# The wait at the end of a one-core transformer block: the wait for all stores on GpSimd's queue instead of SyncE's

## The chip, the cores and the metric

One core of one Trainium2 chip runs the whole kernel as one program. The metric is device time in microseconds (us). The times of before are three: 149.34 us median, 149.03 lowest, 149.63 highest. The profiled execution took 149.33 us.

## The reference

A layer norm of `x` (2048 tokens, 448 features) feeds two branches, and both are added to `x`. All tensors are bfloat16.

```python
xn = _layernorm(x, axis=-1)
return x + _A_ref(xn, A_wqkv, A_w_phi, A_wo) + _B_ref(xn, B_w1, B_b1, B_w2)
```

Branch A is a linear attention with 16 heads of 28 features: `q`, `k` and `v` come from one projection, `q` and `k` pass through a small matrix per head, and the feature map is the softmax of that and of its negative. Numerator and denominator are sums over all tokens, their quotient goes through `wo`. Branch B is a dense layer of 448 to 1792 features with bias, a Mish activation, and a dense layer back to 448.

## The kernel before, in words

The 2048 tokens stand as 16 tiles of 128 tokens. Layer norm runs on pairs of tiles; the normalised pairs are transposed; TensorE makes `k`, `v` and `q` of each pair and the first dense layer (`ffn1`); ScalarE applies the exponentials and Mish; GpSimd scales the feature map of `k`; then TensorE makes numerator and denominator of each tile (`nd`), the projection by `wo` (L845) and the second dense layer (`ffn2`, L828). The last two add into the same PSUM bank of a tile. VectorE adds that bank to `x` (L793) and writes the sum into the tile `x_all`, from where it is stored. The order of the whole program is written out by hand in a list of step names (`ORDER`), whose end is `... g15 stt14 sto6 stt15`: `g15` is the second dense layer of token tile 15, `stt14` the store of tile 14, `sto6` that of tiles 12 and 13, `stt15` that of tile 15.

Tile 15 is the last one. Its columns 0 to 383 are made first; its columns 384 to 447 come from 18 narrow matmuls behind them (L807 to L810, `last_columns`), and VectorE adds these with an instruction of its own (L814). It is therefore stored in two pieces: the first by ScalarE's DMA queue, the second by SyncE's (L856). All other stores are issued by SyncE (L859). There are ten stores: `sto0` to `sto6`, `stt14`, and the two of `stt15`.

Each operation is recorded with what it reads and writes. `resolve` works out from that which earlier operations each one must wait for; each DMA has a semaphore of its own, which its landing raises to 16. `emit` then writes the engines' programs: for each operation its waits, and then the instruction itself.

```python
    def emit(self, name, eng):
        for o in self.ops[name]:
            for d in o.deps:
                eng.wait_ge(d.sem, d.count)
            ins = o.fn(eng)
```

The waits are L131 in the profile. The last recorded operation, behind the whole order, is an empty one on SyncE that reads everything the ten stores wrote (L928). So it waits for ten semaphores. In the built program that is five instructions of SyncE's queue that each wait for two semaphores; four of them count as L131, and the fifth, which waits for the two stores of tile 15, as L928. There is no further instruction for the empty operation. SyncE's last other instruction is the store of tile 15's last columns (L856). GpSimd's last instruction is a copy of 64 by 64 elements (L820), which waits for two loads of `wo` and which one of the narrow matmuls reads (L808).

When an engine has come to the end of its program, the engines meet: the trace holds the times at which one more semaphore, number 2, is raised, which the kernel does not use. It is raised in rounds of nine: two rounds ahead of the program's first instruction, and two around and behind its last.

Of the kernel before, what the change touches and what calls it, by code (L numbers as in the profile page):

```python
# [17 lines left out]
NT = S // P  # L18
# [20 lines left out]
class Program:  # L39
# [13 lines left out]
    def op(self, eng, fn, r=(), w=(), dma=False, tag="", after=()):  # L53
        o = Op()
        o.tag, o.parts = tag, None
        o.eng, o.fn, o.dma, o.needed, o.count, o.sem = eng, fn, dma, False, 0, None
        o.idx = len(self.ops[eng])
        deps = list(after)
        for res in list(r) + list(w):
            if res[0] == "ps":  # L60
                deps += [a for e, a in self.psum.get(res, {}).items() if e != eng]
        for res in r:
            if res[0] != "ps":
                deps += self.writers.get(res, [])
        for res in w:
            if res[0] != "ps":
                deps += [d for d in self.writers.get(res, []) if d.dma or dma or d.eng != eng]
                deps += [d for d in self.readers.get(res, []) if d.dma or dma or d.eng != eng]
        for res in r:
            if res[0] == "ps":  # L70
                self.psum.setdefault(res, {})[eng] = o
            else:
                self.readers.setdefault(res, []).append(o)
        for res in w:
            if res[0] == "ps":
                self.psum.setdefault(res, {})[eng] = o
            else:
                self.writers[res] = [o]
                self.readers[res] = []
        o.deps = deps  # L80
        self.ops[eng].append(o)
        self.order = getattr(self, "order", [])
        self.order.append(o)
        return o
# [54 lines left out]
def bass_parallel_sum__linear_kernel_hedgehog__dense_activation_mish__prompt_kernel(  # L139
    nc, A_x, A_wqkv, A_w_phi, A_wo, B_x, B_w1, B_b1, B_w2, out  # L140
):
    es = ExitStack()
    with es:
        _kernel(es, nc, A_x, A_wqkv, A_w_phi, A_wo, B_w1, B_b1, B_w2, out)
# [21 lines left out]
def run_order(steps, order):  # L166
    for name in order:
        steps[name]()


def _kernel(es, nc, A_x, A_wqkv, A_w_phi, A_wo, B_w1, B_b1, B_w2, out):
# [88 lines left out]
    op, dma = pg.op, pg.dma  # L260
# [508 lines left out]
    LAST = int(ORDER.split()[-1][3:])  # L769
# [155 lines left out]
        add(f"z{n}", warm, n)  # L925

    run_order(steps, ORDER.split())
    op("SP", lambda e: e.nop(), r=[("dram", t) for t in range(NT)] + [("draml", LAST)])  # L928

    pg.resolve()  # L930
    for name, eng in (("SP", nc.sync), ("POOL", nc.gpsimd), ("PE", nc.tensor), ("ACT", nc.scalar), ("DVE", nc.vector)):
# [29 lines left out]
```

## Time and profile before

| | |
|---|---|
| median of three runs | 149.34 us (149.03 to 149.63) |
| the profiled execution | 149.33 us |
| its span, first to last recorded instruction | 148.1 us |
| instructions in it | 3852 |
| TensorE matmul busy | 143.2 us (97%) |
| VectorE busy | 102.8 us (69%) |
| ScalarE busy | 74.5 us (50%) |
| GpSimd busy | 38.7 us (26%) |
| granted TensorE clock | 1.00 |

The page calls TensorE's matmuls PE, VectorE DVE, ScalarE ACT, GpSimd POOL and SyncE SP. A q behind a name is the engine's sequencer, which waits on semaphores and issues DMAs; its instructions do not count as busy time. The span ends with the last recorded instruction, so the profiled execution has 1.2 us outside of its span, ahead of the first instruction or behind the last.

### The profile page before, as it was taken

What the parts mean: (1) busy time and instruction counts of PE and PEld (TensorE: products, weight loads), DVE (VectorE), ACT (ScalarE), POOL (GpSimd) and SP (SyncE); (2) the same over time, 40 slices, a digit from 0 to 9 for tenths busy, and PEclk for the clock granted to TensorE, in tenths of its full rate; (3) what the DMA queues carried; (4) which work ended last, traced back from release to release, by engine and by line L of the source; (5) the groups of instructions that cost most, each with busy time, mean ns of one, the idle gap of its engine ahead of it and who ended that gap; (6) DMA issues with size and microseconds to landing.
All of it is one profiled execution on the core that took longest, in us unless ns stands there. A gap on an engine that the chain in (4) does not pass through costs nothing.

```text
span 148.1 us, 3852 instructions
## 1 busy us (share of the span) xinstructions
PE 143.2 (97%) x1669; PEld 75.3 (51%) x1669; DVE 102.8 (69%) x229; ACT 74.5 (50%) x91; POOL 38.7 (26%) x53
## 2 busy tenths in 40 slices
PE   6799999999999999999999999999999999999994
PEld 2375555465554554444444455545555555555473
DVE  0699898996999940407698879639993999940062
ACT  4987999869999999657756753003000000000000
POOL 4414465179999993000000000000000000000000
DMA  4997777799699179399956033020004050533005
GB/s 133 243 284 221 155 143 150 118 170 328 112 192 188 37 40 145 63 228 309 194 121 127 0 66 62 12 55 0 7 2 122 0 128 0 124 62 124 4 0 186
DMA packets 39965, 17.23 MB, mean 116 GB/s; under 512 B 33933, under 2 KB 39181, under 8 KB 39949
## 3 DMA queue, kind: packets, MB, share of 16 engines
q1 hardware_dynamic: 39776, 16.89, 54.6%
q8 instruction: 13, 0.21, 0.6%
q10 hardware_dynamic: 172, 0.10, 0.2%
q14 instruction: 4, 0.02, 0.1%
HBM read 7.02 MB, written 1.84 MB: 60 GB/s over the span
## 4 chain that ended last, share of the span: by engine, by line
PE 93%; DMA 2%; DVE 1%; ACT 1%; POOL 1%; issue 0%
PE PS L423 51%; PE PS L828 29%; PE PS L845 7%; PE PS L722 3%; DMA x_all<-in_A_x_dram 2%; PE PS L649 2%; PE PS L580 1%; DVE xn L497 1%; PE PS L505 1%; ACT junk L458 1%; POOL rstd L473 0%; ACT junk L453 0%; DVE x_all L793 0%; PE PS L556 0%; POOL lnv L470 0%
## 5 line engine op out<-in xcount | busy, mean ns | idle before, releaser
L423 PE MATMUL PS<-xnT,W 64*128 64x512 bf16 x392 | 44.8, 377 | 0.0
L828 PE MATMUL PS<-W,actT 128*128 128x448 bf16 (+1 forms) x224 | 42.9, 351 | 0.0
L699 ACT ACTIVATE actT<-PS,b1T 128x1024 bf16<-128x1024 f32 x28 | 29.8, 1112 | 22.1 <-PE PS L423 22.1
L828 PEld LDWEIGHTS PS<-W,actT 128*128 128x128 bf16 x224 | 21.5, 98 | 19.8 <-issue 0.3
L423 PEld LDWEIGHTS PS<-xnT,W 64*128 64x128 bf16 x392 | 18.4, 94 | 21.5 <-PE PS L423 1.9
L630 POOL TENSOR_TENSOR actT<-actT,rSk 128x896 bf16<-128x896 bf16 x16 | 26.6, 1699 | 5.3 <-DVE rSk L628 5.3
L793 DVE TENSOR_TENSOR x_all<-PS,x_all 128x448 bf16<-128x448 f32 (+1 forms) x16 | 9.2, 614 | 15.1 <-PE PS L845 10.5
L626 DVE TENSOR_REDUCE Sk<-actT 128x32 f32<-128x896 bf16 x16 | 16.6, 1037 | 1.1 <-ACT actT L618 1.1
L618 ACT ACTIVATE actT<-PS 128x896 bf16<-128x896 f32 x16 | 13.7, 920 | 2.0 <-PE PS L423 1.9
L423 PE MATMUL PS<-Wpk,xnT 64*128 64x448 bf16 x112 | 13.3, 349 | 0.0
L423 PE MATMUL PS<-Wkv,xnT 64*128 64x448 bf16 x112 | 13.0, 349 | 0.0
L423 PE MATMUL PS<-Wpq,xnT 64*128 64x448 bf16 x112 | 12.6, 349 | 0.0
L738 DVE COPY Sq<-PS 128x16 f32<-128x16 f32 x32 | 4.0, 167 | 12.0 <-PE PS L722 12.0
L462 DVE BATCH_NORM_STATS2 stats<-x_all 128x6 f32<-128x448 bf16 x14 | 8.4, 601 | 3.4 <-DMA x_all<-in_A_x_dram 3.4
L746 DVE TENSOR_TENSOR v_all<-v_all 128x464 f32<-128x464 f32 x16 | 10.3, 642 | 0.6
L742 DVE TENSOR_TENSOR v_all<-PS,Sq 128x464 f32<-128x464 f32 x16 | 10.3, 642 | 0.5
L749 DVE TENSOR_TENSOR xn<-v_all,rden 128x448 bf16<-128x448 f32 x16 | 10.0, 625 | 0.6
L744 DVE TENSOR_TENSOR v_all<-PS,Sq 128x464 f32<-128x464 f32 x16 | 10.1, 630 | 0.0
L680 ACT ACTIVATE actT<-PS 128x896 bf16<-128x896 f32 x10 | 8.6, 930 | 0.1
L423 PEld LDWEIGHTS PS<-Wpk,xnT 64*128 64x128 bf16 x112 | 5.6, 94 | 5.0 <-issue 0.4
L423 PEld LDWEIGHTS PS<-Wkv,xnT 64*128 64x128 bf16 x112 | 5.7, 94 | 4.7 <-ACT actT L618 0.2
L423 PEld LDWEIGHTS PS<-Wpq,xnT 64*128 64x128 bf16 x112 | 5.6, 94 | 4.8 <-ACT actT L680 0.2
(83 smaller groups left out, 118.0 us busy)
## 6 DMA issues: line engine op xcount, KB each, us to landing
W<-in_B_w_dram SPq DMA_DIRECT2D x1, 1568.0 KB, 7.8
out_dram<-x_all SPq DMA_DIRECT2D x7, 224.0 KB, 2.2
W<-in_B_w_dram SPq DMA_DIRECT2D x1, 1344.0 KB, 6.9
x_all<-in_A_x_dram SPq DMA_DIRECT2D x4, 224.0 KB, 2.9
x_all<-in_A_x_dram SPq DMA_DIRECT2D x2, 448.0 KB, 4.5
Wkv<-in_A_wqkv_dram SPq DMA_DIRECT2D x2, 336.0 KB, 4.8
Wo<-in_A_wo_dram SPq DMA_DIRECT2D x2, 336.0 KB, 6.3
W<-in_B_w_dram SPq DMA_DIRECT2D x2, 224.0 KB, 3.7
```

Source lines behind the costliest of these rows:

```text
L423: ins = e.matmul(o, lhs(c, k), rhs(c, k), start=first and n == at[par][0], stop=last and n == at[par][-1])
L618: op("ACT", lambda e, s=s: e.activation(E_of(u)[:, s, :, :], two(b, D), ACT.Exp, scale=1.0 if s == 0 else -1.0), r=[pb(b), pb(b + 1)], w=[ ...
L626: op("DVE", lambda e: e.tensor_reduce(Sk[u][:, s, :], Eh(), AX.X, ALU.add), r=[("E", u, s)], w=[("Sk", u, s)], tag=f"Sk{u}.{s}")
L630: op("POOL", lambda e: e.tensor_tensor(Eh(), Eh(), ap_on(rSk[u][:, s, 0:1], [[1, 2 * H], [0, DH]]), ALU.mult), r=[("E", u, s), ("rSk", u, ...
L699: op("ACT", lambda e: e.activation(actT[:, fc, q * 1024:(q + 1) * 1024], bank(b, 2), ACT.Mish, bias=b1T[:, fc:fc + 1]), r=[("b1T",), pb(b) ...
L742: op("DVE", lambda e: e.tensor_tensor(tv(t1[i]), num(0), sx(1), ALU.mult), r=[pb(b), pb(b + 1), ("Sq", i, 1)], w=[("t1", i)], tag=f"ta{t}")
L744: op("DVE", lambda e: e.tensor_tensor(tv(t2), num(1), sx(0), ALU.mult), r=[pb(b), pb(b + 1), ("Sq", i, 0)], w=[("t2",)], tag=f"tb{t}")
L746: op("DVE", lambda e: e.tensor_tensor(t1[i], t1[i], t2, ALU.add), r=[("t1", i), ("t2",)], w=[("t1", i)], tag=f"tc{t}")
L749: op("DVE", lambda e: e.tensor_tensor(o_sb[(t // 2) % 2][:, t % 2, :].rearrange("p (h d) -> p h d", d=DH), t1[i][:, :, 0:DH], ap_on(rden[i ...
L793: op("DVE", lambda e: e.tensor_tensor(x_all[:, t, 0:n], bank(b)[:, 0:n], x_all[:, t, 0:n], ALU.add), r=[pb(b), ("x", t)], w=[("out", t)], ...
L828: ins = e.matmul(bank(b)[:, 0:width(t)], actT[:, fc, tok(t)], W2[:, fc, 0:width(t)], start=first and fc == 0, stop=last and fc == FC - 1)
L845: ins = e.matmul(bank(b)[:, 0:w], oT_of(u)[lo:hi, cc * P:(cc + 1) * P], Wo[lo:hi, cc, 0:w], start=first and n == at[par][0], stop=last and ...
```

## The change

The empty operation that waits for the ten stores is recorded on GpSimd instead of SyncE. The same ten semaphores are waited for, in the same pairs and the same order, by five instructions of GpSimd's queue behind its copy L820; SyncE's queue ends with the store of tile 15's last columns. The instructions that work, and those that issue DMAs, stand in the same order as before on all five engines, with the same waits.

```diff
     run_order(steps, ORDER.split())
-    op("SP", lambda e: e.nop(), r=[("dram", t) for t in range(NT)] + [("draml", LAST)])
+    op("POOL", lambda e: e.nop(), r=[("dram", t) for t in range(NT)] + [("draml", LAST)])
```

## The prediction

> **What bounds the kernel now.** I read the page first, for the span and its chain; then the chain of waits of the last ten microseconds; then the queue's side of the same stretch (timeline, waits and single lines of SP and POOL); and last the trace's semaphore records, since the change touches semaphores alone. The page's span and the chain that ended last:
>
> ```profile
> span 148.1 us, 3852 instructions
> PE 143.2 (97%) x1669; PEld 75.3 (51%) x1669; DVE 102.8 (69%) x229; ACT 74.5 (50%) x91; POOL 38.7 (26%) x53
> PE 93%; DMA 2%; DVE 1%; ACT 1%; POOL 1%; issue 0%
> ```
>
> TensorE bounds all but the two ends. The chain from 138 us on shows where it hands over:
>
> ```profile
> 139.12 3.97 PE PS L845 x41
> 143.09 2.42 PE PS L828 x14
> 145.51 0.02 issue
> 145.53 0.56 DVE x_all L793
> 146.09 0.19 DVE x_all L814
> ```
>
> Behind the last addition, which ends at 146.28, there is only the tail: two stores of tile 15, their landing, the wait for it, and the closing of the program. The timeline of SP and the one of ACT show the issues, the list of DMA issues the landings:
>
> ```profile
> 144.15 1.36 SPq L859 DMA_DIRECT2D out_dram<-x_all  x3
> 146.31 0.33 SPq L856 DMA_DIRECT2D out_dram<-x_all  x1
> ...
> 146.12 0.39 ACTq L856 DMA_DIRECT2D out_dram<-x_all  x1
> ...
> out_dram<-x_all ACTq DMA_DIRECT2D x1, 96.0 KB, 1.7
> out_dram<-x_all SPq DMA_DIRECT2D x1, 16.0 KB, 1.7
> ```
>
> SP's piece starts at 146.31 and lands 1.7 later, at 148.0, and that is the end of the span. Who waits for it, by the waits of SP from 140 us on and the single line L928:
>
> ```profile
> SPq L928 <- DMA out_dram<-x_all: 0.9, 1, 0.9
> SPq L856 <- DVE x_all L814: 0.8, 1, 0.8
> SPq L131 <- DMA out_dram<-x_all: 0.3, 1, 0.3
> ...
> L928 SPq EVENT_SEMAPHORE  x1: 168/168/168, 147.9 to 147.9; - x1
> ```
>
> L928 is the fifth of the five waits. It starts at 147.9, when the first of its two semaphores is full, and its 168 ns end the span. The other engines' queues have long been at their end by then; GpSimd's most of all:
>
> ```profile
> 75.74 0.23 POOL L820 COPY WoB<-Wo 64x64 bf16<-64x64 bf16 x1 [18.96 <-DMA Wo<-in_A_wo_dram]
> ```
>
> What follows the span no view prints, but the trace has the times of each semaphore's increments. Semaphore 2 is raised nine times in a row at each meeting of the engines. Its last rounds, and the last increments of the semaphores that three of the waits need (us from the span's start):
>
> ```
> semaphore 2, last round ahead of the program:
>    -0.371  -0.337  -0.298  -0.254  -0.231  -0.119  -0.081  -0.047   0.000
> first round behind it:
>   146.196 146.769 146.807 146.851 148.174 148.218 148.256 148.291 148.337
> second round:
>   149.151 149.186 149.224 149.268 149.291 149.389 149.427 149.461 149.508
> store of tile 15, ACT's piece, landed 147.870; SP's piece 148.031
> last load of wo, landed 75.622; GpSimd's wait for it ended 75.652
> ```
>
> I read the first round behind the program so: the five engines raise the semaphore one after the other on the way up, and four of them again on the way down. The fifth up is SP, since it alone is still waiting, and it raises 0.120 us behind the end of its wait (148.054). The first is TensorE (its last matmul ends at 146.02), the second ScalarE (its issue ends at 146.51). GpSimd and VectorE are the third and the fourth. They follow ScalarE at 0.038 and 0.044 us, because they had nothing left to do.
>
> **What the change does, part by part.** Its sum is made against the profiled execution: 149.33 us, of which 148.05 are span and 1.28 lie around it; that is 0.01 from the median of the three runs.
>
> *What is removed from SP.* Five semaphore instructions behind its last issue. SP then comes to the program's end at 146.64, the end of that issue, instead of 148.05. That gains nothing by itself: SP raises fifth, and GpSimd, ahead of it, now raises only when the stores have landed. No DMA moves: the issues of SP and ACT and the waits ahead of them are the same, so the landing at 148.031 stays. Cost 0; the cover is not work but the same landing.
>
> *What is added to POOL, early.* The five waits stand behind the copy of 75.74, so GpSimd's queue stands at the first of them from 76 us on. Nothing is queued behind them but the end of the program, and nobody waits for GpSimd after the copy: TensorE's narrow matmuls read its result 70 us later. That a waiting GpSimd slows nobody is seen before that copy: its queue waited 19.0 us there, and the chain has TensorE alone all through it. Two rows of the whole chain:
>
> ```profile
> 28.30 22.69 PE PS L423 x226
> ...
> 59.30 7.90 PE PS L423 x72
> ```
>
> Cost 0. Four of the waits are over by 147.16 on SP and will be so on POOL, since their stores land by then and each such instruction is short:
>
> ```profile
> L131 POOLq EVENT_SEMAPHORE  x5: 17/17/458, 4.3 to 75.2; - x5
> L131 SPq EVENT_SEMAPHORE  x4: 28/28/268, 146.7 to 146.9; - x4
> ```
>
> *The last wait, woken.* On SP it ends 0.023 us behind the landing (148.031 to 148.054). On POOL the one wait that a landing ended in sight ended 0.030 us behind it (75.622 to 75.652; it is the 458 ns in the row above). So +0.007.
>
> *From the wait to the raise.* SP took 0.120. TensorE took 0.176 (146.020 to 146.196), ScalarE 0.261 (146.508 to 146.769). GpSimd's is not in sight, because it raised late, behind ScalarE. From below: a semaphore instruction of SP follows the one before it at about 0.07 (268 ns and three instructions between 146.693 and 147.162), so 0.07; from above ScalarE's 0.261. I take TensorE's 0.176, the middle one of three engines, so +0.06 (ends -0.05 and +0.14).
>
> *The place in the round.* SP, the fifth, had four raises behind its own: 148.174 to 148.337, 0.163. GpSimd is third, so two more come behind it. In the second round, where no one waits for a store, the third raise to the ninth takes 0.284 (149.224 to 149.508), the fourth to the ninth 0.240. So +0.12, or +0.08 if GpSimd is the fourth. [...]
>
> The sum: 0.007 + 0.06 + 0.12 = 0.19, rounded to +0.2. What stands behind the round (the clearing of semaphores between 148.29 and 148.93, the second round) moves with it. So 149.33 + 0.2 = **149.5 us**, 0.13% more. No change could be told from a measurement of this kernel below 0.5%, or 0.75 us.
>
> **The rivals.**
>
> *GpSimd has something to finish at its program's end (slower).* Until now that lay under 72 us of nothing. Place: between the end of GpSimd's wait and its raise. Price from the trace: in the round ahead of the first one shown, semaphore 2 was raised at -7.401, -3.505 and -2.703, so an engine once came 0.80 behind its forerunner, and another 3.90. Had GpSimd's closing the shorter of these, it would be 0.80 instead of 0.12, and the sum 0.007 + 0.68 + 0.12 = 0.81: 150.1 us, just beyond 0.5%. It decides from a closing of 0.74 on. For it: nothing in the trace shows GpSimd's closing. Against it: those gaps stand where a program is set up, and the three engines whose closing can be seen take 0.12 to 0.26. Chance 0.08.
>
> *The empty operation is a GpSimd instruction and no wait of its queue.* Then it would go down to the engine behind the wait. The trace has the price: the copy starts 0.09 behind the wait ahead of it (75.652 to 75.74) and takes 0.23, so up to 0.32 more, 149.8 us. [...] Against it: on SP the operation was the fifth EVENT_SEMAPHORE itself, L928, and POOL's are the same kind, at 17 ns. Chance 0.05.
>
> *The way down is shorter, or SP's closing was longer than it looks (faster).* At best all that lies between the end of the wait and the end of the round goes, 148.054 to 148.337, 0.28: 149.05 us. For it: SP, done early, does its part in advance, and one 8 KB packet of queue 14, which the page counts among instructions, is seen from 148.185 to 148.553, just behind SP's raise; it could come earlier. Against it: a round needs all five, and the clearing that ends last (148.927) is another engine's. Chance 0.06. It is no gain that could be measured.
>
> *The change doesn't do what it says.* The closing might wait for the stores by itself, or the time be taken where the round no longer counts. Then the time is that of before, 149.3 us. Against it: in before the round stood still from 146.851 until 148.174, for SP and its wait. Chance 0.03.
>
> **How the numbers follow.** The forecast has the rest, 0.78, and its own ends: -0.05 + 0.08 + 0.007 = +0.04 and +0.14 + 0.12 + 0.007 = +0.27, so 149.4 to 149.6 on the profiled run. The three runs lie from 0.31 below to 0.29 above their median, which is more than the terms. The lower end is the faster case, 149.05, rounded down for that scatter: 149.0. The upper end is the forecast's highest, 149.63 + 0.27 = 149.9, with the second rival's 149.8 inside, rounded up to 150.0; the slower rival's 150.1 is left out. Over 0.5% slower is above 150.1: most of the slower rival, 0.07, and 0.01 for scatter. Over 0.5% faster is below 148.6: no case gives it, 0.02 for scatter. Within 0.5%: 0.90.
>
> **What the profile after would show.** SP's records end with the issue at 146.3; five EVENT_SEMAPHOREs stand on POOL, the last of them ending some 0.03 behind the landing of SP's piece. The span stays at 148.1, since its last record is still that wait. In semaphore 2's first round the third raise (or the fourth) is late instead of the fifth: about 0.18 behind the wait, and the round ends 0.28 behind that raise, not 0.16. The forecast's steps would be wrong if the raise came over 0.3 behind the wait (the slower rivals), if a record of POOL other than a semaphore's stood at the end (the second), if the fifth raise were still the late one, or if TensorE's part of the span moved, which nothing here touches.

## The result, and the profile after

The changed kernel takes 150.66 us (six runs, 150.5 to 151.36), the kernel before 149.33 us beside it (six runs, 149.0 to 149.67). The ratio is 1.0087, with a 95% interval of 1.0066 to 1.0108: slower by some 1.3 us, more than the 0.5% that can be told apart. The profiled execution took 150.61 us, 1.28 us more than that of before. Kernel times here and below are medians, and three single executions of three of the kernels below, which took 190, 302 and 528 us, are left out of them.

The page of the changed kernel, its span, busy times and the chain that ended last by engine:

```profile
span 148.8 us, 3852 instructions
PE 143.9 (97%) x1669; PEld 75.6 (51%) x1669; DVE 102.6 (69%) x229; ACT 74.5 (50%) x91; POOL 38.7 (26%) x53
...
PE 96%; DVE 1%; POOL 0%; issue 0%; POOLq 0%
```

The span is 0.8 us longer, at the same number of instructions. The chain of waits from 138 us on (start, duration, what):

```profile
139.22 3.97 PE PS L845 x41
143.19 2.42 PE PS L828 x14
145.61 0.02 issue
145.63 0.56 DVE x_all L793
146.19 0.19 DVE x_all L814
```

Every piece has its length of before and stands 0.10 us later. That tenth arises at the start: the first load of `x` lands at 3.58 instead of 3.38, the first long run of the projections' matmuls begins at 10.53 instead of 10.33, and half of the delay is made good later. The start varies from run to run (the last matmul ends between 145.86 and 146.71 in the profiles below), so I do not count it to the change. 1.2 of the 1.3 us lie behind 146.4. The stores of tile 15, by the list of DMA issues (queue, size, us to landing):

```profile
out_dram<-x_all ACTq DMA_DIRECT2D x1, 96.0 KB, 2.4
out_dram<-x_all SPq DMA_DIRECT2D x1, 16.0 KB, 2.4
```

Both were 1.7 before. They are the same transfers, issued by the same engines at the same distance from the additions. The waits, by their lines (count, shortest/median/longest ns, first and last start):

```profile
L131 POOLq EVENT_SEMAPHORE  x9: 17/43/11049, 4.5 to 146.7; - x9
...
L928 POOLq EVENT_SEMAPHORE  x1: 176/176/176, 148.7 to 148.7; - x1
```

The five waits are GpSimd's now, and L928 still ends the span. The rest stands in the trace's records of semaphores and packets, which no view prints (us from the span's start):

```
changed kernel
GpSimd's 2nd wait ended      146.221
         3rd wait started    146.605, ended 146.648
         4th wait ended      147.269
         5th wait (L928)     148.656 to 148.832
queue 14, one packet of 8192 bytes   147.319 to 147.867    (before: 148.185 to 148.553)
ACT's piece, its 16 increments: first 147.755, 15th 147.967, 16th 148.633   (before: 147.654, 147.854, 147.870)
SP's piece,  its 16 increments: first 147.947, 15th 148.158, 16th 148.803   (before: 147.828, 148.011, 148.031)
semaphore 2, first round:   146.294 146.866 149.365 149.409 149.432 149.529 149.568 149.602 149.649
second round:               150.437 150.471 150.509 150.554 150.577 150.675 150.714 150.748 150.794
```

Three things are to be seen. Each of the two landings raises its store's semaphore sixteen times, in both kernels. Fifteen of the sixteen increments come as they did before, and the sixteenth 0.65 to 0.67 us behind the fifteenth (before: 0.016 and 0.020), in both stores. A packet of queue 14, which the page of the profile counts among instructions (`q14 instruction: 4, 0.03, 0.1%`: packets, MB, share), lies between the issue of these stores and their late landing (147.319 to 147.867). And GpSimd's raise of semaphore 2, the third, comes 0.533 behind its wait (148.832 to 149.365), after which the round takes 0.284.

In numbers: 0.10 (start), 0.68 (landing: 2.40 instead of 1.72 behind SP's issue), 0.01 (waking), 0.41 (0.533 instead of 0.120 to the raise), 0.12 (0.284 instead of 0.163 for the rest of the round): 1.32. What comes behind the round is 0.03 shorter, and 1.28 were measured.

### The profile page after: what moved, and what is told of

Same layout as the page of the kernel before. It is cut to its first block, busy times and chain, and to the rows that moved or that the text cites. A ratio compares the mean times of both kernels' runs of the same rounds, so it can differ in the third digit from the quotient of the medians.

```text
span 148.8 us, 3852 instructions
## 1 busy us (share of the span) xinstructions
PE 143.9 (97%) x1669; PEld 75.6 (51%) x1669; DVE 102.6 (69%) x229; ACT 74.5 (50%) x91; POOL 38.7 (26%) x53
## 4 chain that ended last, share of the span: by engine, by line
PE 96%; DVE 1%; POOL 0%; issue 0%; POOLq 0%
PE PS L423 51%; PE PS L828 29%; PE PS L845 7%; PE PS L364 3%; PE PS L722 3%; PE PS L649 2%; PE PS L580 1%; DVE xn L497 1%; PE PS L505 1%; DVE x_all L793 0%; POOL v_all L339 0%; PE PS L556 0%; DVE x_all L814 0%; DVE b1T L512 0%; PE PS L693 0%
```

## The experiments

Because the start varies by more than some of the effects, each profile is also read by its tail: from the end of the last matmul to the last increment of semaphore 2. The tail is 3.49 us before (146.020 to 149.508) and 4.68 in the changed kernel (146.117 to 150.794), 1.19 more. The tails and ratios of all profiles stand in one table behind them. I call the time from the end of an engine's last instruction to its raise its closing. My theory, A, was that GpSimd's longer queue crosses a point at which the next 8 KB of its instructions come in, as the packet of queue 14 (its fetch point), and that this packet holds back one of the sixteen increments of each of the last stores; the rivals were that waiting itself delays the stores (B), and further ones as they came up.

### Half of the wait each

```diff
-    op("SP", lambda e: e.nop(), r=[("dram", t) for t in range(NT)] + [("draml", LAST)])
+    op("SP", lambda e: e.nop(), r=[("dram", t) for t in range(NT) if t != LAST])
+    op("POOL", lambda e: e.nop(), r=[("dram", LAST), ("draml", LAST)])
```

> SyncE waits for the eight stores ahead of tile 15, GpSimd for the two of tile 15 alone, so GpSimd's queue is four instructions shorter than in the changed kernel. Theory A (GpSimd's queue crosses a point at which the next 8 KB of instructions are fetched, and that packet holds up one of 16 DMA engines just when the last stores land; besides, GpSimd takes 0.53 from its wait to its raise, and raises third): no 8 KB packet of queue 14 between 146.5 and 148, the last stores land 1.7 behind their issue, the raise stays 0.53 behind the wait; 149.33 + 0.41 + 0.12 = 149.9. Theory B (an engine that stands waiting on the stores' semaphores makes them land later): landings stay at 2.4, 150.6. The forecast's own figure for GpSimd's closing would give 149.5.

Measured: 150.54 us beside 149.53 (ratio 1.0056, 1.0035 to 1.0078), tail 0.86 longer. Both pieces landed in 1.7 again, though GpSimd waited for them, which speaks against B:

```profile
out_dram<-x_all ACTq DMA_DIRECT2D x1, 96.0 KB, 1.7
out_dram<-x_all SPq DMA_DIRECT2D x1, 16.0 KB, 1.7
```

The packet stood at 150.225, behind the landings and the raise. But the raise came 0.877 behind the wait (148.427 to 149.304), not 0.533, and the time was not A's 149.9. The missing 0.34 us fits what the changed kernel shows between GpSimd's second and third wait: the third starts 0.384 behind the end of the second, though one of its stores had landed at 121, and elsewhere the start follows at 0.044. A's crossing is then also a stall of GpSimd's queue of 0.34, and it lies two instructions behind the copy L820, wherever these are: here the one wait and the first instruction of the closing, so that the stall falls into the closing. This was a reading after the fact. The next runs test the place of the crossing; that the 0.34 of this run is the same stall stays inferred.

### Fills on GpSimd, to move the crossing

Theory A's own test: the wait of the changed kernel, with eight tiny fills that GpSimd does at 76 us.

```diff
+    pad = sb("pad", [P, 16], FP32)
+    for i in range(8):
+        op("POOL", lambda e, i=i: e.memset(pad[:, i:i + 1], 0.0), r=[("WoB",)], w=[("pad", i)])
-    op("SP", lambda e: e.nop(), r=[("dram", t) for t in range(NT)] + [("draml", LAST)])
+    op("POOL", lambda e: e.nop(), r=[("dram", t) for t in range(NT)] + [("draml", LAST)])
```

> The changed kernel with eight tiny fills of a scratch tile on GpSimd behind its copy, at 76 us, where it is idle. Theory A: GpSimd crosses the fetch point at about 76 us, the 8 KB packet moves there, the last stores land 1.7 behind their issue, 149.9. Theory B: GpSimd waits as in the changed kernel, landings 2.4, 150.6.

Measured: 150.26 us beside 149.53 (ratio 1.0043, 1.0026 to 1.0059), tail 0.54 longer, which is 0.41 for the closing and 0.12 for the round. The 149.9 expected had the same two terms, on 149.33 for the kernel before; on the 149.53 measured beside it they give 150.06. The 8 KB packet moved to 76.980. GpSimd's waits, by their lines:

```profile
L131 POOLq EVENT_SEMAPHORE  x9: 17/209/11055, 4.4 to 146.8; - x9
...
L931 POOLq EVENT_SEMAPHORE  x1: 168/168/168, 148.1 to 148.1; - x1
```

And the landings, by its DMA issues:

```profile
out_dram<-x_all ACTq DMA_DIRECT2D x1, 96.0 KB, 1.7
out_dram<-x_all SPq DMA_DIRECT2D x1, 16.0 KB, 1.7
```

GpSimd stands in the same waits, in the same pairs, as in the changed kernel, and the stores land in 1.7: B is refuted. Adding eight instructions to GpSimd took 0.65 us off the tail. The third wait now starts 0.044 behind the second (146.323 to 146.367), and the raise comes 0.533 behind the last.

### The early waits on GpSimd as well

```diff
+    op("POOL", lambda e: e.nop(), r=[("dram", t) for t in range(NT) if t != LAST])
     op("SP", lambda e: e.nop(), r=[("dram", t) for t in range(NT)] + [("draml", LAST)])
```

> SyncE waits for all ten stores as in the kernel before; GpSimd waits too, for the eight stores ahead of tile 15. GpSimd ends at 147.3, a microsecond ahead of SyncE. Theory A: GpSimd crosses the fetch point behind its four waits, the 8 KB packet stands near 147.3, the last stores land 2.4 behind their issue although SyncE waits for them; GpSimd's raise, 0.53 behind its last wait, is hidden; 149.33 + 0.68 = 150.0. Theory B: GpSimd does not wait for the last stores, so they land 1.7 behind their issue; 149.3.

Measured: 149.52 us beside 149.53 (1.0002, 0.9988 to 1.0017). I missed here: I had the crossing behind the fourth wait. The packet stood at 136.078, and the third wait started 0.399 behind the second (135.007 to 135.406): the crossing is behind the second, as the first experiment had suggested, and in this kernel's pairs the second needs a store that had landed by 135. So the packet met nothing, and the landings stayed at 1.7. GpSimd's raise came 0.533 behind its last wait (147.220 to 147.753), hidden under SyncE's.

### The collision made on purpose, with SyncE last

GpSimd waits for six of the early stores. The first two of its three waits are those of the changed kernel.

```diff
+    op("POOL", lambda e: e.nop(), r=[("dram", t) for t in range(4, 15)])
     op("SP", lambda e: e.nop(), r=[("dram", t) for t in range(NT)] + [("draml", LAST)])
```

> SyncE waits for all ten stores as before; GpSimd waits for six of the early ones, in pairs of which the first two are those of the changed kernel. GpSimd's fetch point lies between the second and the third wait in the runs so far, so it is crossed when the store of tiles 8 to 11's second half lands, near 146.1. Theory A: the 8 KB packet stands at 146.8 to 147.5; where it overlaps the last stores' packets (147.0 to 147.5) one of 16 increments of both comes some 0.6 late, landings 2.2 to 2.4, and the time is 150.0 to 150.2 beside 149.53 of the kernel before, with SyncE last as ever. Theory C (the packet is harmless, and the last stores landed late in the changed kernel since GpSimd waited for them): landings 1.7, 149.5.

Measured: 150.55 us beside 149.53 (1.0065, 1.0038 to 1.0093), tail 0.56 longer; the time is above the 150.0 to 150.2 expected, which the tail would give. SyncE waits last and closes as ever, by its lines of waits:

```profile
L131 SPq EVENT_SEMAPHORE  x4: 28/28/274, 147.2 to 147.4; - x4
...
L929 SPq EVENT_SEMAPHORE  x1: 175/175/175, 148.9 to 148.9; - x1
```

And the landings, by its DMA issues:

```profile
out_dram<-x_all ACTq DMA_DIRECT2D x1, 96.0 KB, 2.3
out_dram<-x_all SPq DMA_DIRECT2D x1, 16.0 KB, 2.3
```

The packet stood from 147.720 to 148.247. The fifteenth increment of SP's piece came at 148.521, the sixteenth at 149.072; of ACT's at 148.348 and 148.903. That the packet of GpSimd's instructions, and not GpSimd's waiting for the stores, makes them late is shown by this run and the fills together: landings of 2.3 with the packet at 147.720 and SyncE waiting, 1.7 with the packet at 76.980 and GpSimd waiting.

### The same number of instructions, other pairs

```diff
-    op("SP", lambda e: e.nop(), r=[("dram", t) for t in range(NT)] + [("draml", LAST)])
+    op("POOL", lambda e: e.nop(), r=[("dram", t) for t in range(NT) if t != LAST])
+    op("POOL", lambda e: e.nop(), r=[("dram", LAST), ("draml", LAST)])
```

> GpSimd waits for all ten stores in five instructions, as in the changed kernel, but in other pairs: the first two need stores that land by 134.4, and the third already needs ScalarE's piece of tile 15. Theory A: the fetch point between the second and the third is crossed at 134.4, the 8 KB packet stands near 135.5, landings 1.7; closing 0.53 and the longer round stay; two waits are left behind the last landing instead of one, +0.05; 149.53 + 0.41 + 0.12 + 0.05 = 150.1. Theory C (GpSimd's waiting makes the last stores land late): landings 2.4, 150.8.

Measured: 150.12 us beside 149.43 (1.0049, 1.0030 to 1.0068), tail 0.63 longer. A's sum was 0.41, 0.12 and 0.05; the two waits left behind the last landing cost 0.13 instead of 0.05 (148.536 to 148.689, where before has 0.023), and the rest of the tail is 0.03 shorter. The packet stood at 136.062, 1.07 behind the end of the second wait. GpSimd's waits by their line:

```profile
L131 POOLq EVENT_SEMAPHORE  x8: 17/30/7520, 4.3 to 148.6; - x8
```

And the landings, by its DMA issues:

```profile
out_dram<-x_all ACTq DMA_DIRECT2D x1, 96.0 KB, 1.7
out_dram<-x_all SPq DMA_DIRECT2D x1, 16.0 KB, 1.7
```

### The changed kernel again

The file of the changed kernel, as it is.

> The changed kernel once more, beside the same runs of the kernel before as the other two. Theory A: the 8 KB packet near 147.3 again and landings of 2.2 to 2.4; 149.53 + 1.2 = 150.7. If the landing had been chance: 1.7, and 150.1.

Measured: 151.16 us beside 149.43 (1.0113, 1.0095 to 1.0131), above the 150.7 expected; tail 1.13 longer. The packet stood at 147.480 to 148.073, the third wait started 0.377 behind the second, and the landings repeat:

```profile
out_dram<-x_all ACTq DMA_DIRECT2D x1, 96.0 KB, 2.4
out_dram<-x_all SPq DMA_DIRECT2D x1, 16.0 KB, 2.3
```

Beside the same runs of the kernel before, other pairs are 1.0 us faster than this (150.12 and 151.16), 0.50 by the tails.

### The wait on the other three engines

In place of the changed line, `"ACT"`, `"DVE"` or `"PE"`; for ScalarE also with the fills above.

> The wait for all ten stores is ScalarE's instead of GpSimd's. Theory A: the queues of GpSimd and SyncE are both short, ScalarE's has no fetch point here, landings 1.7; ScalarE raises second, 0.26 behind its wait; 149.33 + 0.14 + 0.16 = 149.6. Theory B (any other engine than SyncE): landings 2.4, 150.3.

> ScalarE waits for all ten stores, and GpSimd has eight tiny fills behind its copy at 76 us. With ScalarE's wait alone the round behind the program stood still for 0.29 between its sixth and seventh raise. Theory A (that is GpSimd crossing its fetch point inside the round): with the fills it crosses at 76 us, the sixth and seventh raise are 0.04 apart, and the time falls by 0.25 against ScalarE's wait alone, to 149.7 (0.16 for the longer round above the kernel before's 149.53). Theory C (the gap is the price of ScalarE waiting last): the gap stays, 150.0.

> The wait for all ten stores is VectorE's. Theory A: GpSimd, one place ahead of VectorE, has raised and crossed its fetch point before the stores land, so no stall in the round; VectorE is fourth, one more raise than SyncE, +0.08; its closing some 0.11 to 0.18: 149.6 to 149.7. Theory C (any engine but SyncE costs half a microsecond): 150.0.

> The wait for all ten stores is TensorE's. Theory A: TensorE is first in the round, so all eight other raises come behind its own (0.36 in the round where nobody waits, 0.20 more than behind SyncE's), GpSimd crosses its fetch point within the round (+0.25), closing 0.18 (+0.06): 149.53 + 0.5 = 150.0. Theory C (a fixed price for any engine but SyncE): the same as ScalarE's and VectorE's run.

Measured: ScalarE 150.01 beside 149.53 (1.0023, 1.0007 to 1.0038), tail 0.40 longer; ScalarE with fills 149.63 (1.0005, 0.9988 to 1.0022), 0.15; VectorE 149.91 (1.0018, 1.0000 to 1.0035), 0.08; TensorE 150.04 (1.0029, 1.0008 to 1.0049), 0.49. All landings were 1.7. The first rounds of semaphore 2:

```
ScalarE             146.035 148.006 148.045 148.088 148.111 148.208 148.496 148.531 148.578
ScalarE with fills  146.888 148.853 148.891 148.935 148.958 149.056 149.094 149.128 149.175
VectorE             146.741 147.312 147.350 148.746 148.769 148.867 148.905 148.939 148.986
TensorE             148.160 148.194 148.233 148.276 148.299 148.397 148.693 148.727 148.774
```

The raise that is late is ScalarE's second, VectorE's fourth and TensorE's first, and in the changed kernel it was GpSimd's third: so the order on the way up is TensorE, ScalarE, GpSimd, VectorE, SyncE, as I had taken it. With ScalarE or TensorE last, the seventh raise comes 0.29 behind the sixth, and that is GpSimd's on the way down; with the fills it is 0.04. The fills, which move the crossing to 76 us, take ScalarE's gap away: so GpSimd raises, crosses its fetch point, and is late for its second raise. TensorE's gap I read in the same way. For ScalarE alone I had left this out, and expected 149.6. VectorE and SyncE come behind GpSimd in the round, so GpSimd has crossed while it waits for them: with VectorE last the seventh raise is again 0.038 behind the sixth (148.867 to 148.905), and so it is in the kernel before (148.218 to 148.256). VectorE's time of 149.91 is above what its tail gives (149.6); its interval of 0 to 0.5 us holds both. My closing for ScalarE, 0.26, was too long: it raises 0.109 behind its wait (147.897 to 148.006).

### Two controls

The fills with the wait left on SyncE, and the changed kernel with the fills at 76 us and one more tiny fill behind the wait:

```diff
+    op("POOL", lambda e: e.memset(pad[:, 8:9], 0.0), r=[("dram", LAST)], w=[("pad", 8)])
```

> The kernel before with the eight tiny fills on GpSimd at 76 us. Theory A: the packet moves from 148.2 to 77, where nothing waits for it; SyncE last as before; 149.5, the same as the kernel before. Theory C (the fills, not the moved packet, changed something in the runs that had them): another time than before's.

> The changed kernel with the eight fills at 76 us, and one more tiny fill behind the wait for the stores. It asks what GpSimd's 0.53 from its last instruction to its raise is. Theory D1 (a fixed closing of GpSimd's queue): the raise is 0.53 behind the last fill's start or end, so 0.6 to 0.75 behind the wait; 150.2 to 150.3. Theory D2 (it comes only when the last instruction was a wait): the raise is some 0.3 behind the wait; 149.9.

Measured: the fills alone 149.69 beside 149.43 (1.0005, 0.9991 to 1.0019), tail 0.03 shorter: the packet stood at 76.674, and no difference can be told. The last fill 150.64 (1.0078, 1.0057 to 1.0098), above the 150.2 to 150.3 expected, with a tail 0.69 longer, as expected. The fill ended at 148.723, the raise came 0.512 later, near the 0.533 behind a wait: GpSimd's closing here does not depend on the last instruction's being a wait (D1).

### All runs

| kernel | ratio | SP's last store, issue to landing | last engine: wait to raise | rest of the round | tail, against 3.49 |
|---|---|---|---|---|---|
| changed | 1.0087 | 2.40 | GpSimd 0.533 | 0.284 | +1.19 |
| changed, again | 1.0113 | 2.34 | GpSimd 0.533 | 0.283 | +1.13 |
| half each | 1.0056 | 1.72 | GpSimd 0.877 | 0.285 | +0.86 |
| changed, fills | 1.0043 | 1.72 | GpSimd 0.533 | 0.284 | +0.54 |
| changed, other pairs | 1.0049 | 1.72 | GpSimd 0.533 | 0.284 | +0.63 |
| early waits on both | 1.0002 | 1.70 | SyncE 0.121 | 0.163 | -0.02 |
| collision, SyncE last | 1.0065 | 2.28 | SyncE 0.115 | 0.163 | +0.56 |
| fills, SyncE last | 1.0005 | 1.71 | SyncE 0.121 | 0.163 | -0.03 |
| ScalarE | 1.0023 | 1.72 | ScalarE 0.109 | 0.572 | +0.40 |
| ScalarE, fills | 1.0005 | 1.72 | ScalarE 0.110 | 0.322 | +0.15 |
| VectorE | 1.0018 | 1.72 | VectorE 0.139 | 0.240 | +0.08 |
| TensorE | 1.0029 | 1.72 | TensorE 0.187 | 0.614 | +0.49 |
| changed, fills, one behind | 1.0078 | 1.71 | GpSimd 0.512 (from the fill) | 0.284 | +0.69 |

Only the profiled execution of each kernel has a trace. In three kernels of four to six executions each (changed again, collision, and one fill behind) the ratio stands for 0.4 to 0.6 us more than the tail gives; where that lies is open. No version beats the kernel before. SyncE is the right engine here: it stands last on the way up, so the fewest raises come behind its own (0.163 us, against 0.240 to 0.614 for the other engines), and it closes in 0.12.

## Why the prediction was wrong

The forecast was 149.5 us with a range to 150.0, and 150.66 was measured. Step by step:

- **TensorE bounds all but the ends, and nothing moves there.** Right.
- **What is removed from SP: the landing at 148.031 stays, cost 0.** This step failed, and with it **What is added to POOL, early: cost 0**. I asked only whom the five instructions make wait. But they also make GpSimd's program longer, and a point that by my reading lay in its closing came to lie between its second and third wait. There GpSimd's queue stalls for 0.34 us (the third wait starts 0.384 behind the second instead of 0.044), hidden under the landings, and 0.7 us later the 8 KB packet (147.319 to 147.867) lay among the last stores' transfers. The landing came 2.40 behind the issue instead of 1.72. Cost 0.68, of 1.19. I had the packet in sight, in the faster rival: "it could come earlier". It did, by 0.87 us, and that was the harm.
- **The last wait, woken: +0.007.** Right: 0.029 behind the landing (148.803 to 148.832) instead of 0.023.
- **From the wait to the raise: +0.06, at most +0.14.** The term was mis-sized. Behind a wait GpSimd takes 0.53 in all six runs whose fetch point lay elsewhere, and 0.877 in the run where I infer the crossing to lie in its closing. The bounds came from other engines and did not hold GpSimd's; ScalarE's 0.261, the upper one, is not even its own closing, which is 0.109 where it waits last. The slower rival, that GpSimd has something to finish, was right in place and sign; it had 0.80, and decided alone only from 0.74 on. What fills the 0.53 stays open: no record stands in it.
- **The place in the round: +0.12.** Right, 0.284 instead of 0.163, and GpSimd is third.
- **The empty operation as a GpSimd instruction, and the change that does not do what it says.** Both refuted: five EVENT_SEMAPHOREs stand on POOL, and the round waits for the last (from 146.866 to 149.365).

I had named as a sign against the forecast a raise over 0.3 behind the wait; it is there. The late landing I had not named, since I took it for fixed: I had the span at 148.1 still, and it is 148.8.

Why the packet makes an increment late is not shown: the trace names no DMA engine, neither for the packet nor for an increment, so that both belong to the same one of sixteen, as theory A had it, is a guess. What is shown is that one of sixteen increments is late, by 0.55 to 0.67 us, in the three runs with the packet in that stretch, whose packets took 0.53 to 0.59, and in none of the others. The cost of the crossing is hidden in the kernel before (packet at 148.185, behind the last landing at 148.031) and wherever GpSimd crosses early: with SyncE last and the packet at 76.674 the tail was within 0.03 us of that of before. Near the end it was not hidden: 0.25 us in the round of raises with ScalarE last (0.29 instead of 0.04), and 0.68 in the landing.

## What to carry to other kernels

What ended this program is the round behind the last engine's raise, so whoever holds the last wait should close fast and stand late in the round of raises: here SyncE took 0.12 and 0.163 us, GpSimd 0.533 and 0.284. An instruction can cost nothing where it stands and still shift what its queue does later: five waits on GpSimd moved the 8 KB packet from 148.185 to 147.319, eight fills ahead of them to 76.980. Near the end, look where that packet falls. The last wait here was over only behind the sixteenth increment of its store (148.803, 0.645 behind the fifteenth), so read the last increments one by one when a landing is late.

## What the runs showed of the hardware

- Each engine's closing had its own length here: 0.11 (ScalarE), 0.12 (SyncE), 0.14 (VectorE), 0.19 (TensorE), 0.53 (GpSimd) from the last wait to the raise. VectorE's and TensorE's rest on one profile each.
- The round of raises behind the last wait takes 0.02 to 0.10 a step, but for the 0.29 ahead of the seventh raise with ScalarE or TensorE last. It goes up through TensorE, ScalarE, GpSimd, VectorE and SyncE, as the late raise of each run shows. That gap puts GpSimd's second raise in the seventh place; that the others come down in the reverse order too is my reading.
- GpSimd's queue stood still for 0.33 to 0.36 between its second and third wait in the runs where I read the crossing there (0.377 to 0.399 from wait to wait, against 0.044); the 8 KB packet followed 0.67 to 0.71 behind the wait that came next (146.605 to 147.319, 146.769 to 147.480, 135.406 to 136.078), and took 0.31 to 0.59 us itself. In all five runs with the crossing there, the packet started 1.07 to 1.11 behind the end of GpSimd's second wait behind its copy.
- Two stores of 96 and 16 KB, otherwise landing in 1.7 us, took 2.3 to 2.4 with that packet among theirs.
